# Key and query weights turned by DMAs straight from DRAM, and the order of the work as a table

## The chip, the cores and the metric

The kernel runs on one core of a Trainium2 chip. The time is the device time of one execution in microseconds (us), and less is better. The engines are TensorE (PE; its weight loads are shown apart as PEld), VectorE (DVE), ScalarE (ACT), GpSimd (POOL) and SyncE (SP). SP and ACT issue the DMAs of this kernel.

## The reference

Two layers, each made of a linear attention (A) and a gated feed-forward block (B), on one sequence of 2048 rows of 512 numbers in bfloat16. Each block reads a layer norm of x and adds its output to x. Both layers use the same weights.

```python
x = x + A(layernorm(x)); x = x + B(layernorm(x))      # twice

def A(x):                                  # 32 heads of 16
    q, k, v = split(x @ wqkv)              # wqkv: 512 x 1536
    pq, pk = q @ w_phi, k @ w_phi          # per head, 16 x 16
    phi_q = [softmax(pq), softmax(-pq)]    # over 16, so 32 features
    phi_k = [softmax(pk), softmax(-pk)]
    kv = phi_k.T @ v;  z = sum(phi_k)      # per head, over all 2048 rows
    return (phi_q @ kv) / (phi_q @ z + 1e-6) @ wo

def B(x):
    return (relu(x @ W_gate) * (x @ W_up)) @ W_down    # 512 -> 1376 -> 512
```

The sum kv runs over all rows, so no output of A exists before every row has had its keys and values.

## The kernel before

x stays in SBUF as 16 tiles of 128 rows, in 4 chunks of 4 tiles. A matmul needs the normalised tile turned (columns on the partitions). `Norm` takes the statistics of a tile (L385 on DVE, or a square on ACT, L408, with the sum taken in passing at L494), forms the reciprocal root on POOL (L393 to L444), normalises on ACT (L456), DVE or POOL (L468), and turns the tile by a DMA issued by SP, one tile (L486) or two at a time (L482), or by PE with a copy behind it (L478, L479).

The head matrices `w_phi` are multiplied into the weights first: `feature_weights` builds Wk2 = Wk x blockdiag(w_phi), and Wq2 likewise. The fold (L361) wants Wk and Wq turned. Wk is loaded with plain rows, turned by 16 small matmuls on PE (L348) and copied out of PSUM by ACT (L304) and DVE (L306); then come four folds and four casts into `Wk2`. Wq is loaded with plain rows (L238) and turned by two DMAs out of SBUF (L334). The block diagonal `Wblk` is made on DVE (L324) from w_phi and a mask `M8`.

Then, for each tile: keys (L637), the two exponentials (L642), values (L590) and their cast (L304), the sums of the features over 16 on DVE (L609 whole, L619 one sign at a time, L615 after a first addition on POOL, L606), reciprocal (L651), scaling on POOL or DVE (L657) and the running sum kv in PSUM (L679). Queries (L721, L725) have the same sums, a reciprocal (L730), a product (L732), scaling (L739) and a turn by DMA (L741). Attention (L758 to L809) and the feed-forward block (`glu`, L520 to L572) follow chunk by chunk. 17 matmuls of zeros (`wake`, L315) are given to PE at the start.

The order on every engine is fixed before the kernel runs. Each step is an `op` of a `Plan`, with the engine, an assumed duration, what it reads and writes and, for things that come from DRAM, an assumed time of arrival (`X_IN`, `WK_IN` and so on). Before, `Plan.order` played these durations through and let each engine take the ready step with the highest rank: the longest path to the end plus a number per group of steps (`RANK`). Strings in `STEP` say which engine takes which variant of a step (`kr0` is the way of the key sums of layer 0, tile by tile; `wev` the engine of each copy of the weights; `xm0` whether tiles are turned in pairs). Each engine runs its list in order, so a step that waits holds all behind it on that engine, DMA issues included.

Of the kernel before, what the change touches and what calls it, by code (L numbers as in the profile page):

```python
# [8 lines left out]
P = 128  # L9
# [51 lines left out]
class Plan:  # L61
# [10 lines left out]
    def op(self, eng, occ, fn, reads=(), writes=(), holds=(), lat=0.0, at=0.0, group=None, port=False, long=False):  # L72
# [4 lines left out]
        base, slope = RANK.get(f"{o.group}.{eng}") or RANK[o.group]  # L77
        o.bias = base - slope * o.i_in
# [19 lines left out]
    def order(self):  # L98
        for o in self.ops:
            for p in o.preds:  # L100
                p.succs.append(o)
        for o in reversed(self.ops):
            o.rank = o.cost + o.lat + max([s.rank + hop(o.eng, s.eng) for s in o.succs], default=0.0)
        free = {k: [0.0] * n for k, (pool, n) in self.kinds.items()}
        engines = sorted({o.eng for o in self.ops})
        busy = {e: 0.0 for e in engines}
        ready = {e: [] for e in engines}
        for o in self.ops:
            o.wait, o.t0 = len(o.preds), o.at
            if not o.wait:  # L110
                ready[o.eng].append(o)
        seq, left, now, shut = [], len(self.ops), 0.0, 0.0
        while left:
            moved, later = False, []
            for e in engines:
                if busy[e] > now + 1e-9:
                    later.append(busy[e])
                    continue
                best = None
                for o in ready[e]:  # L120
                    if o.t0 > now + 1e-9:
                        later.append(o.t0)
                        continue
                    if o.port and shut > now + 1e-9:
                        later.append(shut)
                        continue
                    ok = True
                    need = {}
                    for b in o.bufs:
                        if b.slot is None:  # L130
                            need[b.kind] = need.get(b.kind, 0) + 1
                    for k, n in need.items():
                        got = [t for t in free[k] if t is not None]
                        if len(got) < n:
                            ok = False
                        else:
                            t = sorted(got)[n - 1]
                            if t > now + 1e-9:
                                later.append(t)
                                ok = False  # L140
                    if ok and (best is None or (o.rank + o.bias, -o.i) > (best.rank + best.bias, -best.i)):
                        best = o
                if best is None:
                    continue
                o = best
                ready[e].remove(o)
                moved, left = True, left - 1
                o.start, end = now, now + o.cost
                busy[e] = now + o.occ
                if o.long:  # L150
                    shut = end
                later.append(busy[e])
                for b in o.bufs:
                    if b.slot is None:
                        b.slot = min((i for i, t in enumerate(free[b.kind]) if t is not None),
                                     key=lambda i: free[b.kind][i])
                        free[b.kind][b.slot] = None
                        b.end = 0.0
                    b.left -= 1
                    b.end = max(b.end, end + o.lat + FREE)  # L160
                    if not b.left:
                        free[b.kind][b.slot] = b.end
# [770 lines left out]
```

## Time and profile before

| | us |
|---|---|
| median of 3 runs | 382.19 (382.05 to 382.74) |
| profiled execution | 380.87 |
| its span, first to last instruction | 379.1 |
| PE busy | 368.0 |
| DVE busy | 272.1 |
| ACT busy | 211.0 |
| POOL busy | 139.5 |
| mean granted TensorE clock | 0.995 |

In the rows of the profile, `out<-in` names the tiles with their numbers left out: `b` stands for all buffers of the kinds b1, b2 and b4, `ps` for the PSUM banks, `Wk` and `Wq` for Wk2 and Wq2. A row of the timeline gives start, length, engine, line, operation and, in brackets, how long the engine had been idle and what ended that. A row of the table of stretches gives, for a stretch of time, its length, then for each engine the busy time with the number of instructions in parentheses, then the granted PE clock, the share of the DMA engines and GB/s. `SPq` and `ACTq` are the issuing of DMAs by SP and ACT, and a row of DMA issues ends with the time from issue to landing. Rows of groups give the busy time in all, the mean of one in ns, and the idle time before them.

### The profile page before, as it was taken

What the parts mean: (1) busy time and instruction counts of PE and PEld (TensorE: products, weight loads), DVE (VectorE), ACT (ScalarE), POOL (GpSimd) and SP (SyncE); (2) the same over time, 40 slices, a digit from 0 to 9 for tenths busy, and PEclk for the clock granted to TensorE, in tenths of its full rate; (3) what the DMA queues carried; (4) which work ended last, traced back from release to release, by engine and by line L of the source; (5) the groups of instructions that cost most, each with busy time, mean ns of one, the idle gap of its engine ahead of it and who ended that gap; (6) DMA issues with size and microseconds to landing.
All of it is one profiled execution on the core that took longest, in us unless ns stands there. A gap on an engine that the chain in (4) does not pass through costs nothing.

```text
span 379.1 us, 6873 instructions
## 1 busy us (share of the span) xinstructions
PE 368.0 (97%) x2435; PEld 190.8 (50%) x2435; DVE 272.1 (72%) x606; ACT 211.0 (56%) x436; POOL 139.5 (37%) x272
## 2 busy tenths in 40 slices
PE   8699999999999999999999999999999999999996
PEld 4245545666445454444454455576655444454444
DVE  5999999999789725636992688999985592532232
ACT  4899878752598241238476377986725135124600
POOL 3799876903366000134360446545311021000000
PEclk9899999999999999999999999999999999999999
DMA  8999816449585100141232020656977014020011
GB/s 255 252 219 212 211 39 138 47 91 173 96 153 100 29 15 2 28 57 29 47 52 55 3 55 2 124 104 86 164 153 112 0 28 112 0 28 30 1 43 55
DMA packets 98403, 32.23 MB, mean 85 GB/s; under 512 B 88800, under 2 KB 98368, under 8 KB 98368
## 3 DMA queue, kind: packets, MB, share of 16 engines
q1 hardware_dynamic: 94400, 28.36, 39.8%
q10 hardware_dynamic: 3968, 3.42, 2.9%
q8 instruction: 19, 0.31, 0.4%
q14 instruction: 16, 0.13, 0.1%
HBM read 8.44 MB, written 2.10 MB: 28 GB/s over the span
## 4 chain that ended last, share of the span: by engine, by line
PE 80%; DVE 9%; DMA 4%; POOL 4%; issue 1%; SPq 1%; ACT 0%; ACTq 0%; POOLq 0%
PE ps L540 36%; PE ps L572 19%; PE ps L809 6%; PE ps L721 4%; PE ps L590 4%; PE ps L637 3%; DMA b<-b 3%; PE ps L520 3%; PE q L758 2%; DVE sk L619 2%; POOL b L657 1%; PE ps L315 1%; DVE rk L651 1%; PE q L679 1%; DVE bnst L385 1%
## 5 line engine op out<-in xcount | busy, mean ns | idle before, releaser
L540 PE MATMUL ps<-b,wu 128*128 128x512 bf16 (+2 forms) x400 | 79.4, 337 | 0.0
L540 PE MATMUL ps<-b,wg 128*128 128x512 bf16 (+2 forms) x400 | 78.9, 337 | 0.0
L572 PE MATMUL ps<-wd,b 128*128 128x512 bf16 (+3 forms) x374 | 78.3, 367 | 0.0
L550 ACT CAST b<-ps 128x512 bf16<-128x512 f32 (+2 forms) x100 | 48.9, 505 | 40.6 <-PE ps L540 39.3
L553 DVE SCALAR_TENSOR_TENSOR b<-ps,b 128x512 bf16<-128x512 f32 (+2 forms) x60 | 34.9, 598 | 30.3 <-PE ps L540 29.8
L572 PEld LDWEIGHTS <-b 128*128 128x128 bf16 (+1 forms) x374 | 35.3, 98 | 39.4
L657 POOL TENSOR_TENSOR b<-b,rk 128x1024 bf16<-128x1024 bf16 (+6 forms) x30 | 42.1, 1410 | 33.9 <-DVE rk L651 26.0
L540 PEld LDWEIGHTS <-wg 128*128 128x128 bf16 x400 | 36.2, 98 | 32.9 <-issue 0.2
L540 PEld LDWEIGHTS <-wu 128*128 128x128 bf16 x400 | 36.1, 98 | 31.9
L456 ACT ACTIVATE b<-X,ve,rstd 128x512 bf16<-128x512 bf16 x42 | 33.4, 818 | 26.2 <-POOL ve L444 21.5
L739 POOL TENSOR_TENSOR b<-b,rq 128x512 bf16<-128x512 bf16 x25 | 26.3, 1050 | 31.2 <-DVE rq L732 24.2
L498 DVE TENSOR_TENSOR X<-X,ps 128x512 bf16<-128x512 bf16 (+2 forms) x34 | 22.0, 649 | 21.2 <-PE ps L572 20.6
L725 ACT ACTIVATE b<-ps 128x512 bf16<-128x512 f32 x64 | 33.3, 615 | 6.2 <-PE ps L721 6.1
L408 ACT ACTIVATE sq<-X 128x512 bf16<-128x512 bf16 x32 | 20.0, 626 | 28.5 <-DVE X L494 26.2
L637 PE MATMUL ps<-Wk,b 128*128 128x512 bf16 x128 | 31.5, 388 | 4.0 <-DMA b<-b 4.0
L642 ACT ACTIVATE b<-ps 128x512 bf16<-128x512 f32 x64 | 33.2, 612 | 1.2 <-PE ps L637 1.2
L494 DVE SCALAR_TENSOR_TENSOR X<-ps,X 128x512 bf16<-128x512 f32 x32 | 21.7, 684 | 13.4 <-PE ps L572 12.5
L809 PE MATMUL ps<-wo,b 128*128 128x512 bf16 x128 | 30.9, 379 | 0.1
L590 PE MATMUL ps<-wkv,b 128*128 128x512 bf16 x128 | 30.9, 384 | 0.0
L721 PE MATMUL ps<-Wq,b 128*128 128x512 bf16 x128 | 30.9, 379 | 0.0
L557 DVE TENSOR_TENSOR b<-b,b 128x512 bf16<-128x512 bf16 (+2 forms) x40 | 14.1, 373 | 22.3 <-ACT b L550 21.9
L546 ACT ACTIVATE b<-ps 128x512 bf16<-128x512 f32 (+2 forms) x40 | 19.8, 496 | 15.1 <-PE ps L540 15.1
(84 smaller groups left out, 463.8 us busy)
## 6 DMA issues: line engine op xcount, KB each, us to landing
out_dram<-X SPq DMA_DIRECT2D x15, 128.0 KB, 1.7
X<-in_A_x_dram ACTq DMA_DIRECT2D x3, 512.0 KB, 7.6
b<-b SPq DMA_TRANSPOSE x87, 3.2
wd<-in_B_W_down_dram SPq DMA_DIRECT2D x5, 256.0 KB, 3.2
wu<-in_B_W_up_dram SPq DMA_DIRECT2D x8, 160.0 KB, 3.3
wg<-in_B_W_gate_dram SPq DMA_DIRECT2D x8, 160.0 KB, 2.9
wkv<-in_A_wqkv_dram ACTq DMA_DIRECT2D x2, 512.0 KB, 5.1
wq<-in_A_wqkv_dram ACTq DMA_DIRECT2D x1, 512.0 KB, 8.3
```

What stands on the lines that cost most here:

```text
L456: pl.op("ACT", 0.72, lambda to=to, t=t, j=j: nc.scalar.activation(out=to(), in_=st.X[:, t, :], func=AF.Identity, scale=rstd[:, j:j + 1], b ...
L540: nc.tensor.matmul(ps[:], lhsT=wt[:, b, f * P:(f + 1) * P], rhs=xnT[:, lo:hi, b, :], start=(b == 0), stop=(b == NDB - 1))
L550: pl.op("ACT", 0.065 + 0.42 * share, lambda ups=ups, ru=ru: nc.scalar.copy(out=ru[:], in_=ups[:]), reads=[(ups, 0)], writes=[(ru, 0)])
L553: pl.op("DVE", 0.08 + 0.53 * share, lambda gps=gps, ru=ru, h=h, cs=cs: nc.vector.scalar_tensor_tensor(out=h[:, cs], in0=gps[:], scalar=0.0 ...
L572: nc.tensor.matmul(yps[:], lhsT=hs[f][:fsz, ti * P:(ti + 1) * P], rhs=st.wd[:fsz, f, cols], start=(f == 0), stop=(f == NFT - 1))
L590: nc.tensor.matmul(vp[:], lhsT=xnT[:, ti, kb, :], rhs=st.wkv[:, kb, D:2 * D], start=(kb == 0), stop=(kb == NDB - 1))
L637: nc.tensor.matmul(ps[:], lhsT=xnT[:, ti, kb, :], rhs=w(kb), start=(kb == 0), stop=(kb == NDB - 1))
L642: pl.op("ACT", 0.49, lambda s=s, ek=ek, pk=pk: nc.scalar.activation(out=ek[:, :, s, :], in_=pk[:].rearrange("p (j x) -> p j x", j=8), func ...
L657: eng.tensor_tensor(out=phiK[:, lo:hi, :, :].rearrange("p j s (f h) -> p (j s) f h", h=4), in0=ek[:, lo:hi, :, :].rearrange("p j s (f h) - ...
L721: nc.tensor.matmul(pq[:], lhsT=xnT[:, ti, kb, :], rhs=st.Wq2[:, kb, :], start=(kb == 0), stop=(kb == NDB - 1))
L725: pl.op("ACT", 0.49, lambda s=s, eq=eq, pq=pq: nc.scalar.activation(out=eq[:, :, s, :], in_=pq[:].rearrange("p (j x) -> p j x", j=8), func ...
L809: nc.tensor.matmul(yps[:], lhsT=turned(b), rhs=st.wo[:, b, :], start=(b == 0), stop=(b == NDB - 1))
```

## The change

- Wk is no longer loaded with plain rows. The first instruction of SP is a transposing DMA from `A_wqkv` in DRAM into `wkT`. The 16 turning matmuls and their four copies are gone, and the folds read `wkT`.
- Wq is no longer loaded with plain rows either. One transposing DMA from DRAM fills `wqT`, a buffer of kind b4. It and all loads that SP issues come after the turn of tile 5 (`turns`).
- The first two X tiles are loaded from ACT's queue instead of SP's; the value weights have a tile of their own, `wvt`.
- The order is a table, `ORDER`: the numbers of all 1867 steps in the order in which they are given out. `RANK` and the search for the best ready step are gone. Some assumed durations and arrivals differ.
- `STEP` differs: 19 wake matmuls instead of 17, of which the table sets eight ahead of the first fold and the others between the folds and among the first keys and values. Tiles 2, 3, 14 and 15 of the first norm are turned singly. In layer 0, the sums of keys and queries take POOL's first addition in 2 places fewer for keys and queries each (an addition per sign) and the one-sign form in more; three products of the queries (`qm0`) go to POOL, four in layer 1 (`qm1`); one normalisation goes from DVE to ACT. In the later norms, squares and normalisations change places between ACT and DVE, and one PE turn of layer 1 becomes a DMA.
- A further way of taking the sums ("T", a DMA turn and eight small matmuls with a mask `M8s`) is added; no letter T stands in the strings. The mask is made all the same, by one reduction on DVE.

```diff
-        base, slope = RANK.get(f"{o.group}.{eng}") or RANK[o.group]
-        o.bias = base - slope * o.i_in
...
+        assert sorted(ORDER) == list(range(len(self.ops)))
+        self.seq = [self.ops[i] for i in ORDER]
+        for o in self.seq:
...
-WF_IN, WK_IN, WV_IN, WQ_IN, LOADED = 3.5, 5.9, 8.6, 13.1, 13.0
-X_IN = [3.25, 3.8] + [7.0] * 2 + [10.1] * 4 + [11.6] * 4 + [14.5] * 4
+WF_IN, WK_IN, WV_IN, WQ_IN, LOADED = 3.6, 5.6, 8.25, 13.0, 13.0
+X_IN = [3.25, 5.2] + [6.75] * 2 + [9.75] * 4 + [11.25] * 4 + [12.75] * 4
...
-    nc.sync.dma_start(out=X[:, 0:1, :], in_=xv[:, 0:1, :])
+    nc.sync.dma_start_transpose(out=wkT[:], in_=A_wqkv[:, D:2 * D])
+    nc.scalar.dma_start(out=X[:, 0:1, :], in_=xv[:, 0:1, :])
     nc.scalar.dma_start(out=wf[:], in_=A_w_phi.rearrange("(b j) d f -> (j d) b f", b=NDB, j=8))
-    nc.sync.dma_start(out=X[:, 1:2, :], in_=xv[:, 1:2, :])
-    nc.scalar.dma_start(out=wkv[:, :, 0:D], in_=wv[:, :, D:2 * D])
+    nc.scalar.dma_start(out=X[:, 1:2, :], in_=xv[:, 1:2, :])
     nc.scalar.dma_start(out=X[:, 2:4, :], in_=xv[:, 2:4, :])
...
-    nc.scalar.dma_start(out=wkv[:, :, D:2 * D], in_=wv[:, :, 2 * D:3 * D])
+    nc.scalar.dma_start(out=wvt[:], in_=wv[:, :, 2 * D:3 * D])
     nc.scalar.dma_start(out=X[:, 4:8, :], in_=xv[:, 4:8, :])
     nc.scalar.dma_start(out=X[:, 8:12, :], in_=xv[:, 8:12, :])
-    nc.scalar.dma_start(out=wq[:], in_=wv[:, :, 0:D])
     nc.scalar.dma_start(out=X[:, 12:16, :], in_=xv[:, 12:16, :])
...
+    st.M8s = const.tile([P, 2, 4], BF16, name="M8s")
+    nc.vector.tensor_reduce(out=st.M8s[:], in_=ident[:].rearrange("p (z k h) -> p z h k", z=2, h=4), axis=AX.X, op=Alu.max)
...
+        if off:
+            part, deps = (lambda m, b: st.wkT[:, b, m * P:(m + 1) * P]), []
+        else:
+            wqT = Buf("b4", [P, NDB, D], BF16)
+            pl.op("SP", 2.0, lambda: nc.sync.dma_start_transpose(out=wqT[:], in_=st.wq_in),
+                  reads=[("turns", 1)], writes=[(wqT, 0)], at=at, lat=3.0)
+            part, deps = (lambda m, b: wqT[:, b, m * P:(m + 1) * P]), [(wqT, 0)]
...
-    "part0": "4111", "part1": "4111", "tB0": "A---", "tB1": "D-DA", "tA": "----", "wev": "AADDAAADADAAAAAA",
-    "xn1": "AAAAADAPDAADAADA", "turn": "A---", "wake": 17, "fuse0": "FFFA", "fuse1": "AFFA", "gate": 1, "sB0": 3,
-    "sB1": 2, "sA": 3, "xB0": "ADADAAAADADADDAA", "xB1": "DADAAADAAAAAAAAD", "xA": "AADDDDDADAADAAAA",
-    "xm0": "22222212", "xmB0": "22221122", "xmB1": "22222222", "xm1": "12222222", "om0": "11112222",
-    "om1": "11222222", "ev0": "AAAAAAAAAAAAAAAA", "ev1": "AAADAADAAAAAADAA", "ks0": "7888076880873788",
-    "ks1": "4322711876616443", "kr0": "H1111P1121221222", "kr1": "P12111111H12P222", "qr0": "1111H11P1122P1PP",
-    "qr1": "111P111111111112", "qs0": "PPPDPPPPDDDPDPPP", "qs1": "PPPPPPPDDPPPPPPP", "ot0": "DDDD-----DDDAA--",
-    "ot1": "--A---AD--A---D-",
+    "part0": "4111", "part1": "4111", "tB0": "A---", "tB1": "D-D-", "tA": "----", "wev": "AADDAAADADAAAAAA",
+    "xn1": "AAAAADAPDAADAAAA", "turn": "A---", "wake": 19, "fuse0": "FFFA", "fuse1": "AFFF", "gate": 1, "sB0": 4,
+    "sB1": 3, "sA": 2, "xB0": "ADADDAADDADADDDD", "xB1": "DADAAADDAAAAADAA", "xA": "AADDDDDAAADAAAAA",
+    "xm0": "11222211", "xmB0": "12222112", "xmB1": "22222221", "xm1": "12221212", "om0": "11112222",
+    "om1": "11222222", "ev0": "AAAAAAAAAAAAAAAA", "ev1": "AAADDAADAAAAAAAA", "ks0": "7888076880873788",
+    "ks1": "4321818154616442", "kr0": "H112121121122222", "kr1": "P111121112122212", "qm0": "DPDDDDDDDDPDDDPD",
+    "qm1": "DDDDPPDDDDPDDPDD", "qr0": "2111H1122121P1PP", "qr1": "111P112122111112", "qs0": "PPPPPPPPDDDPDPPD",
+    "qs1": "DDPDPPPPPPPPPPPP", "ot0": "DDDD------DDAA--", "ot1": "--A-DDAD---DD--A",
 }
-RANK = {
...
+ORDER = (
+    131, 144, 139, 143, 145, 129, 135, 130, 0, 1, 148, 149, 2, 3, 9, 4, 5, 150, 138, 10, 147, 152, 11, 13, 134, 12,
...
-        n = Norm(st, "b4", (1, 1, 2) if c == 0 else (2, 2), STEP["xn1"], STEP["xm0"], X_IN, STEP["turn"] if c == 0 else "")
+        n = Norm(st, "b4", (1, 1, 1, 1) if c == 0 else (2, 2), STEP["xn1"], STEP["xm0"], X_IN, STEP["turn"] if c == 0 else "")
```

`feature_sums`, with the added way "T":

```python
    if how == "T":
        turned = Buf("b2", [P, 8, P], BF16)
        pl.op("SP", 1.25, lambda: nc.sync.dma_start_transpose(out=turned[:], in_=e[:].rearrange("p j s x -> p (j s x)")),
              reads=[(e, 0), (e, 1)], writes=[(turned, 0)], lat=2.0, group=(group, t))
        ...
        pl.op("PE", 0.26, add_up, reads=[(turned, 0)], writes=[(sums, 0), (sums, 1)], group=(group, t))
        return
```

More of the change, by code (lines that the diff above doesn't have):

```diff
@@ L98, in order @@
     def order(self):
[L99 to L103, printed above, removed]
-        free = {k: [0.0] * n for k, (pool, n) in self.kinds.items()}
[L105 to L162, printed above, removed]
-                for s in o.succs:
-                    s.wait -= 1
-                    s.t0 = max(s.t0, end + o.lat + hop(e, s.eng))
-                    if not s.wait:
-                        ready[s.eng].append(s)
-                seq.append(o)
-            if not moved:
-                later = [t for t in later if t > now + 1e-9]
-                assert later, "the plan is stuck"
-                now = min(later)
@@ L176, in emit @@
+        return self.seq
     def emit(self):
```

98 lines of the change are left out of this document (49 added, 49 removed), and 112 rows, old and new, of tables (ORDER, RANK).

## The prediction

> **What bounds the kernel now.** I read the page first (busy rows, slices), then the chain that ended last, then a table of stretches, then PE's instructions in order of time.
>
> ```profile
> span 379.1 us, 6873 instructions
> PE 368.0 (97%) x2435; PEld 190.8 (50%) x2435; DVE 272.1 (72%) x606; ACT 211.0 (56%) x436; POOL 139.5 (37%) x272
> ...
> PE 80%; DVE 9%; DMA 4%; POOL 4%; issue 1%; SPq 1%; ACT 0%; ACTq 0%; POOLq 0%
> ...
> core 0: us, PE busy (x) PEld busy (x) DVE busy (x) ACT busy (x) POOL busy (x), PEclk, DMA share, GB/s
> ...
> 10.40:17.20 6.80, 3.47 (x13) 1.04 (x11) 6.17 (x19) 5.68 (x10) 5.84 (x13) 0.90 0.99 255
> 17.20:22.00 4.80, 4.75 (x24) 2.13 (x25) 4.41 (x11) 4.02 (x8) 4.55 (x9) 0.79 1.18 172
> 22.00:30.00 8.00, 7.20 (x61) 3.80 (x58) 7.53 (x14) 7.33 (x15) 7.77 (x12) 1.00 1.09 245
> 30.00:40.00 10.00, 10.00 (x67) 4.73 (x64) 9.38 (x16) 10.00 (x21) 9.66 (x9) 1.00 0.84 186
> 40.00:50.00 10.00, 9.87 (x102) 5.58 (x102) 10.00 (x21) 8.30 (x17) 7.97 (x5) 1.00 0.67 187
> 50.00:60.00 10.00, 8.90 (x66) 4.11 (x62) 10.00 (x23) 8.69 (x18) 7.99 (x9) 1.00 0.40 80
> 60.00:80.00 20.00, 19.16 (x206) 12.67 (x207) 19.09 (x53) 13.59 (x37) 12.91 (x30) 1.00 0.51 82
> ...
> 130.00:160.00 30.00, 30.00 (x165) 14.53 (x163) 14.56 (x26) 7.93 (x16) 1.51 (x5) 1.00 0.07 14
> ```
>
> PE is busy 97% of the span and 80% of the chain, but not everywhere the bound: the chain's 9% of DVE lie mostly before 60 us. From 130 us it has no hole to speak of: that part only shrinks with PE work. Before 80 us, DVE is as full as PE (10.00 of 10.00 us in both stretches from 40 to 60). PE's loss lies there: of the 69.6 us from 10.4 to 80, 6.25 are idle, and more pass at a lowered clock. By instruction:
>
> ```profile
> 6.59 1.06 PE L348 MATMUL ps<-ident,wkv 128*128 128x128 bf16 x16
> ...
> 10.43 1.02 PE L637 MATMUL ps<-Wk,b 128*128 128x512 bf16 x4
> 14.54 1.04 PE L637 MATMUL ps<-Wk,b 128*128 128x512 bf16 x4 [3.09 <-DMA b<-b]
> ...
> 52.72 0.43 PE L679 MATMUL q<-vext,b 128*128 128x68 bf16 x8 [0.54 <-POOL b L657]
> ...
> 60.14 0.41 PE L758 MATMUL q<-R,b 128*128 128x68 bf16 x8 [0.70 <-DVE b L778]
> ...
> 71.34 1.95 PE L540 MATMUL ps<-b,wu 128*128 128x128 bf16 x32
> ```
>
> The largest hole, 3.09 us, waits for the turned tile 1 of x. Why that is late stands in ACT's order (the first fence is from the timeline: start, length, instruction), and what follows on SP; the last row is a piece of the chain, the flight of the second half of Wq:
>
> ```profile
> 1.83 0.53 ACTq L228 DMA_DIRECT2D X<-in_A_x_dram  x1
> ...
> 4.30 0.98 ACTq L238 DMA_DIRECT2D wq<-in_A_wqkv_dram  x1
> ...
> 6.66 0.81 ACT L456 ACTIVATE b<-X,ve,rstd 128x512 bf16<-128x512 bf16 x1 [2.77 <-POOL ve L444]
> 7.38 1.53 ACT L304 COPY b<-ps 128x512 bf16<-128x512 bf16 x3
> 8.80 1.58 ACT L304 CAST Wk<-ps 128x512 bf16<-128x512 f32 x3
> 10.23 0.86 ACT L456 ACTIVATE b<-X,ve,rstd 128x512 bf16<-128x512 bf16 x1
> 11.11 1.29 SPq L486 DMA_TRANSPOSE b<-b  x1
> ...
> 16.71 2.67 SPq L334 DMA_TRANSPOSE b<-wq  x2
> ...
> 54.01 17.54 SPq L741 DMA_TRANSPOSE b<-b  x7
> ```
> ```profile
> 18.05 3.98 DMA b<-wq
> ```
>
> Tile 1 is normalised at 10.23 only, behind three copies (two of turned Wk, one of turned tile 0) and three casts of the folded Wk. The later waits are set by POOL and DVE (52.72, 60.14).
>
> **The change, part by part.** The sum is made against the profiled execution (380.87 us with 379.1 of span), which is 1.32 below the median of 382.19; I subtract the same gain from the median.
>
> Wk turned from DRAM. Gone: 16 turns on PE (1.06, all ahead of the first keys, so inside the start), two copies on ACT, two on DVE. New: one transposing DMA of 512 KB, first on SP. No row shows one from DRAM. Nearest: the two DMAs b<-wq, the same 512 KB out of SBUF, were issued from 16.71 and landed at 18.05 + 3.98 = 22.03, so 5.3 us. Issued at about 0.8, where SP's first load was, the new one lands near 6.1. Lower end: one of the two alone, 4.0, so 4.8. Upper end, since nothing shows a DRAM source: half that rate, 10.6, so 11.4 (an estimate from these two rows). I take 6.1, the row with the same bytes; the plain load was turned from 6.59.
>
> ACT's new order in the table is: cast of the first quarter of Wk, tile 0, tile 1, copy of turned tile 0, two casts. From 6.1: a fold of four small matmuls 0.4 (16 such took 1.06), a cast 0.53 (1.58 for three), two normalisations of 0.81: tile 1 is done near 8.7 (10.23 + 0.86 = 11.09 before). From there to K of tile 1 took 14.54 − 11.09 = 3.45, so that comes near 12.2 instead of 14.54, 2.3 us earlier. The other casts end near 10.4, so K of tile 0 stays where it is. Break-even for the landing is 6.1 + 2.3 = 8.4.
>
> First X tiles on ACT's queue, Wq's load gone from it. ACT issues four loads ahead of its first activation instead of three, 0.5 more (the 1.83 row), and four behind it instead of five, 0.98 less; ACT's first normalisation waited for POOL until 6.66, so neither shows. Tile 1 of X comes later, behind Wk, tile 0 and the small w_phi: between 0 and 1.5 us, taken as hidden, since its normalisation now has until 7.8; what outlasts that goes straight onto tile 1.
>
> Wake matmuls, 17 to 19, six or more of them now among the first keys and values. They cost nothing while PE waits there; if the holes are gone, 6 x 0.26 = 1.6 (four matmuls of this size in 1.04). They fill holes after which PE ran slow: (1 − 0.90) x 6.8 + (1 − 0.79) x 4.8 = 1.7 us lost between 10.4 and 22. The Trainium skill, "TensorE: Matmul & The Clock Gate" (Part 1), has the clock halved after about 3.4 us of idleness; the trace agrees in kind (3.09 us of hole, then 0.79). By that rule, with every hole split, all 1.7 would come back on PE.
>
> Wq turned from DRAM: one issue in place of two (2.67 on SP), placed behind the turn of tiles 4 and 5; 512 KB either way; 0, within 1 us either way, covered by the keys and values of tiles 2 to 5, which the table sets ahead of its fold. Weight loads: the same 28, now scattered, and the first behind the turn of tiles 4 and 5 and Wq's; two parts of the gate stand behind the first and second query transposes, one of down behind the fourth. Those seven began at 54.01 and took 2.5 each, and a load lands in about 3 (next row): the gate's last part by 62 against the first L540 at 71.34, down's by 67: 0.
>
> ```profile
> wg<-in_B_W_gate_dram SPq DMA_DIRECT2D x8, 160.0 KB, 2.9
> ```
>
> Tiles 2, 3, 14 and 15 turned singly instead of in pairs: two more SP issues of 1.29 (11.11 row), hidden in SP's waits; without that cover each costs 1.29 to the tiles behind it.
>
> Work moved between engines up to 80 us. Rows:
>
> ```profile
> L609 DVE TENSOR_REDUCE sk<-b 128x64 f32<-128x1024 bf16 x16 | 19.0, 1195 | 3.8 <-ACT b L642 3.8
> L619 DVE TENSOR_REDUCE sk<-b 128x32 f32<-128x512 bf16 x24 | 15.2, 658 | 0.4 <-ACT b L642 0.4
> L615 DVE TENSOR_REDUCE sk<-b 128x32 f32<-128x256 f32 x8 | 4.5, 568 | 0.2 <-POOL b L606 0.2
> L732 DVE TENSOR_TENSOR rq<-sq 128x32 bf16<-128x32 f32 x32 | 9.0, 282 | 0.1
> L306 DVE COPY b<-ps 128x512 bf16<-128x512 bf16 x8 | 3.1, 402 | 1.8 <-PE ps L348 1.8
> L468 DVE TENSOR_SCALAR b<-X,mv,rstd 128x512 bf16<-128x512 bf16 x7 | 2.8, 408 | 1.9 <-POOL rstd L395 1.9
> L265 DVE TENSOR_REDUCE M<-ident 128x4 bf16<-128x128 bf16 x1 | 0.3, 268 | 0.0
> L606 POOL TENSOR_TENSOR b<-b 128x256 f32<-128x256 bf16 x19 | 12.7, 679 | 0.4 <-ACT b L642 0.3
> L395 POOL TENSOR_TENSOR rstd<-ve,mhalf 128x2 f32<-128x2 f32 (+1 forms) x19 | 12.8, 673 | 0.1
> L444 POOL TENSOR_TENSOR ve<-u,rstd 128x2 f32<-128x2 f32 (+1 forms) x38 | 7.4, 194 | 1.8
> ```
>
> DVE: two copies less, −0.80; M8s, +0.27; one normalisation to ACT, −0.41; three products to POOL, −0.85; feature sums of keys and of queries, each one or so whole reduction and two half sums less for four single reductions: −1.195 − 2 x 0.568 + 4 x 0.658 = +0.30, twice. Sum −1.2. POOL: four additions less, −2.7; three products of 32 elements, between 0.19 and 0.68 each, taken as 0.2, the row nearest in size, +0.6; one more normalisation group, a power of 0.67 and three small ones of 0.2, +1.3; −0.8. ACT: two copies of 0.51 less, one normalisation of 0.81 more, −0.2. In the second half squares and normalisations move between ACT and DVE beside a full PE: 0, and one turn on PE less.
>
> The sum, from the engine that decides. On PE up to 5.0 come free: 2.3 (tile 1), 1.7 (clock), and about 1.0 of the later holes. But DVE must do its work before PE's stock of GLU matmuls opens at 71.34. It had 6.17 + 4.41 + 7.53 + 9.38 + 10 + 10 + 19.09 = 66.6 busy of 69.6: 3.0 idle, of which I let the earlier keys give half. 1.2 + 1.5 = 2.7 us. Profiled 378.2; median 382.19 − 2.7 = 379.5. Its own bounds: 1.2 (no idle closed) to 4.2 (all), so 378.0 to 381.0.
>
> **The rivals.** (1) Wk lands late, and slower is the end. Place: its cast heads ACT's queue, so tiles 0 and 1 are normalised behind it, and through the turn of tile 1 all of PE waits. It decides from a landing of 8.4 on. At 11.4 K of tile 1 is 3.0 later; less the 1.2 of DVE's work, +1.8: 384.0. For it: no row shows a source in DRAM, and wk competes with X. Against: b<-wq did as much beside other DMAs (the DMA share is 1.18 from 17.2 to 22). Chance 0.12. One page makes it far worse: the Trainium skill, "VectorE: DVE Perf Modes" (The three transpose paths), gives 1309 ns for a 128x128 block by DMA against 390 by TensorE. Estimated by it, 16 blocks in sequence take 20.9 us, Wk lands at 21.7, 13.3 behind the break-even, and the kernel takes 382.2 + 13.3 − 1.2 = 394.3; but b<-wq moved as many blocks in 5.3, so that rule gets 0.01.
>
> (2) Everything hidden: DVE paces the first 80 us wherever PE starts, and the new waits in DVE's order eat its 1.2. 381.0 to 382.6, taken as 381.9. For: 10.00 of 10.00 from 40 to 60. Against: 3.0 idle before. 0.16, half of it within 0.2%.
>
> (3) PE gets all: the table draws GLU work forward, so DVE's fullness costs nothing: 382.19 − 5.0 = 377.2. 0.12; against it, GLU's first matmuls need tile 0's attention, which needs the sums over all sixteen key tiles, and so all of DVE's key work.
>
> (4) The table puts PE behind late engines in the middle. Where there was no hole from 130 on, layer 1's keys now stand singly between GLU matmuls; ten waits like the 0.54 at 52.72 cost 5.4: 384.9. 0.10; against it, DVE has 15.4 us free from 130 to 160.
>
> **How the numbers follow.** The forecast holds 0.49. A measurement tells no change within 0.2%, 0.8 us (381.4 to 383.0). Faster: 0.49 + 0.12 + 0.08 = 0.69; same: 0.08 and a little of (1), 0.10; slower: the rest, 0.21. Range 376.8 to 383.8: it holds (3), (2) and the milder half of (1).
>
> **What would show it.** Right: no L348; the DMA of Wk landed by 7; K of tile 1 by 12.6; PEclk above 0.95 between 10 and 22; DVE still over 95% from 30 to 60; first L540 matmuls 2 to 3.5 us earlier. Wrong: landing after 8.4; first keys earlier but L540 not (2); PE holes after 130 (4); holes at GLU's first matmuls waiting for weight loads.

## The result, and the profile after

The changed kernel takes 384.02 us (median of 8 runs, 382.85 to 384.9); the kernel before took 382.12 beside it (8 runs, 381.5 to 383.69). The ratio is 1.0048, 95% interval 1.0031 to 1.0066: slower by half a per cent, where 379.5 was forecast. The profiled execution took 384.60, that of before 380.87, so the two traces stand 3.7 us apart where the medians stand 1.9 apart; a difference between two traces is read with that in mind all through this section.

The page of the changed kernel (line numbers are now those of its own file), and under it its stretches with the columns of the table shown of before, three wide ones added:

```profile
span 382.9 us, 6693 instructions
PE 366.5 (96%) x2384; PEld 190.5 (50%) x2417; DVE 274.9 (72%) x601; ACT 199.9 (52%) x428; POOL 136.6 (36%) x281
...
PE 81%; DMA 9%; ACT 2%; DVE 2%; issue 2%; POOL 2%; SPq 0%; ACTq 0%; POOLq 0%; DVEq 0%
```
```profile
10.40:17.20 6.80, 6.12 (x28) 2.49 (x28) 6.08 (x17) 5.23 (x10) 4.18 (x14) 1.00 0.54 138
17.20:22.00 4.80, 4.57 (x23) 1.89 (x21) 4.80 (x13) 3.70 (x8) 4.68 (x7) 1.00 1.06 165
...
10.40:22.00 11.60, 10.69 (x49) 4.37 (x49) 10.88 (x29) 8.93 (x17) 8.87 (x20) 1.00 0.76 149
22.00:130.00 108.00, 100.36 (x775) 55.47 (x785) 94.06 (x214) 75.90 (x165) 61.16 (x104) 1.00 0.62 122
130.00:375.00 245.00, 242.87 (x1496) 123.97 (x1514) 161.30 (x337) 110.66 (x241) 61.40 (x135) 1.00 0.29 54
```

The same three wide stretches of the kernel before:

```profile
10.40:22.00 11.60, 8.22 (x37) 3.18 (x36) 10.58 (x28) 9.70 (x17) 10.39 (x21) 0.85 1.07 220
22.00:130.00 108.00, 104.47 (x804) 57.16 (x801) 99.77 (x227) 77.28 (x167) 66.20 (x109) 1.00 0.65 128
130.00:375.00 245.00, 244.89 (x1522) 124.60 (x1520) 154.28 (x327) 118.83 (x244) 59.29 (x124) 1.00 0.29 52
```

PE does less (366.5 against 368.0 busy). Of the chain that ended last, DVE's share fell from 9% to 2%, and that of the DMAs rose from 4% to 9%. PE's idle time, the length of a stretch less its busy time, went from 3.38 to 0.91 between 10.4 and 22, with the clock back at 1.00. That is the gain. From 22 to 130 it went from 3.53 to 7.64, and from 130 to 375 from 0.11 to 2.13; a new wait of 1.60 stands ahead of 10.4. Sum: −2.47 + 4.11 + 2.02 + 1.60 = +5.3, less 1.5 of busy time: the 3.8 by which the span grew.

The main holes in PE's order of time in the changed kernel, each with what ended it, and the first keys (L575) and values (L516); the rows are taken from several views:

```profile
6.43 0.59 PE L287 MATMUL ps<-Wblk,wkT 128*128 128x128 bf16 x4 [1.60 <-DVE Wblk L269]
...
11.27 1.03 PE L575 MATMUL ps<-Wk,b 128*128 128x512 bf16 x4
...
13.14 1.04 PE L516 MATMUL ps<-wvt,b 128*128 128x512 bf16 x4 [0.62 <-DMA b<-b]
14.01 1.89 PE L575 MATMUL ps<-Wk,b 128*128 128x512 bf16 x7
...
26.53 1.90 PE L575 MATMUL ps<-Wk,b 128*128 128x512 bf16 x7 [1.19 <-DMA b<-b]
...
36.68 0.60 PE L575 MATMUL ps<-Wk,b 128*128 128x512 bf16 x2 [0.99 <-DMA b<-b]
109.23 1.04 PE L575 MATMUL ps<-Wk,b 128*128 128x512 bf16 x4 [0.99 <-DMA b<-b]
225.91 1.04 PE L575 MATMUL ps<-Wk,b 128*128 128x512 bf16 x4 [1.01 <-DMA b<-b]
```

Four holes of about one microsecond wait for a turned tile (`DMA b<-b`). Two more, at 54.32 (0.88, POOL) and 61.90 (0.86, ACT), wait for late engines. The turns that end the four are slow ones: issued at 21.81, 31.98, 105.15 and 221.58, they land 4.68, 4.66, 4.03 and 4.28 later, where most of their kind take 2.4 (one tile) or 3.1 (two). Why they are slow is what the experiments had to find.

The start, in a row of DVE's timeline and three of the page's DMA issues (KB each, us from issue to landing):

```profile
5.52 0.76 DVE L269 TENSOR_TENSOR Wblk<-M,wf 128x256 bf16<-128x256 bf16 x2 [1.16 <-DMA wf<-in_A_w_phi_dram]
```
```profile
wkT<-in_A_wqkv_dram SPq DMA_TRANSPOSE x1, 4.8
wf<-in_A_w_phi_dram ACTq DMA_DIRECT2D x1, 16.0 KB, 4.2
b<-in_A_wqkv_dram SPq DMA_TRANSPOSE x1, 5.2
```

Wk is there early, at 5.60. But the 16 KB of w_phi, issued 0.4 behind the turn, need 4.2 us instead of 2.4 and land at 5.42 instead of 3.20, so the first fold starts at 6.43 and the keys of tile 0 at 11.27, 0.84 later than before. PE's first work on tile 1 (its values, then its keys at 14.01) begins at 13.14 instead of 14.54.

### The profile page after: what moved, and what is told of

The parts are those of the page before. It is cut to its first block, busy times and chain, and to the rows that moved or that the text cites. A ratio compares the mean times of both kernels' runs of the same rounds, so it can differ in the third digit from the quotient of the medians.

```text
span 382.9 us, 6693 instructions
## 1 busy us (share of the span) xinstructions
PE 366.5 (96%) x2384; PEld 190.5 (50%) x2417; DVE 274.9 (72%) x601; ACT 199.9 (52%) x428; POOL 136.6 (36%) x281
## 4 chain that ended last, share of the span: by engine, by line
PE 81%; DMA 9%; ACT 2%; DVE 2%; issue 2%; POOL 2%; SPq 0%; ACTq 0%; POOLq 0%; DVEq 0%
PE ps L466 36%; PE ps L498 16%; DMA b<-b 7%; PE ps L751 7%; PE ps L575 5%; PE ps L659 5%; PE ps L516 5%; PE ps L446 2%; PE q L700 2%; PE q L617 1%; DMA wf<-in_A_w_phi_dram 1%; ACT b L580 1%; DVE sk L556 1%; ACT b L382 1%; POOL b L595 0%
## 5 line engine op out<-in xcount | busy, mean ns | idle before, releaser
L479 DVE SCALAR_TENSOR_TENSOR b<-ps,b 128x512 bf16<-128x512 f32 (+2 forms) x70 | 40.5, 605 | 36.5 <-PE ps L466 25.5
L595 POOL TENSOR_TENSOR b<-b,rk 128x1024 bf16<-128x1024 bf16 (+7 forms) x30 | 41.0, 1381 | 45.0 <-DVE rk L589 30.4
L580 ACT ACTIVATE b<-ps 128x512 bf16<-128x512 f32 x64 | 35.9, 613 | 16.2 <-PE ps L575 15.8
L382 ACT ACTIVATE b<-X,ve,rstd 128x512 bf16<-128x512 bf16 x39 | 31.6, 823 | 16.4 <-POOL ve L370 16.4
L663 ACT ACTIVATE b<-ps 128x512 bf16<-128x512 f32 x64 | 34.9, 615 | 8.3 <-PE ps L659 7.2
L575 PE MATMUL ps<-Wk,b 128*128 128x512 bf16 x125 | 31.8, 379 | 4.6 <-DMA b<-b 4.4
L420 DVE SCALAR_TENSOR_TENSOR X<-ps,X 128x512 bf16<-128x512 f32 x36 | 24.3, 681 | 16.0 <-PE ps L498 8.3
L424 DVE TENSOR_TENSOR X<-X,ps 128x512 bf16<-128x512 bf16 (+2 forms) x30 | 19.3, 648 | 21.7 <-PE ps L498 16.1
L334 ACT ACTIVATE sq<-X 128x512 bf16<-128x512 bf16 x36 | 22.9, 636 | 18.8 <-DVE X L420 18.5
L516 PE MATMUL ps<-wvt,b 128*128 128x512 bf16 x124 | 31.8, 379 | 0.9 <-DMA b<-b 0.6
L546 DVE TENSOR_REDUCE sq<-b 128x64 f32<-128x1024 bf16 x19 | 22.5, 1199 | 0.0
L720 DVE TENSOR_TENSOR b<-q,dd 128x512 bf16<-128x512 f32 x32 | 21.8, 681 | 0.3
```

Source lines behind the costliest of these rows:

```text
L382: pl.op("ACT", 0.72, lambda to=to, t=t, j=j: nc.scalar.activation(out=to(), in_=st.X[:, t, :], func=AF.Identity, scale=rstd[:, j:j + 1], b ...
L479: pl.op("DVE", 0.08 + 0.53 * share, lambda gps=gps, ru=ru, h=h, cs=cs: nc.vector.scalar_tensor_tensor(out=h[:, cs], in0=gps[:], scalar=0.0 ...
L516: nc.tensor.matmul(vp[:], lhsT=xnT[:, ti, kb, :], rhs=st.wvt[:, kb, :], start=(kb == 0), stop=(kb == NDB - 1))
L575: nc.tensor.matmul(ps[:], lhsT=xnT[:, ti, kb, :], rhs=w(kb), start=(kb == 0), stop=(kb == NDB - 1))
L580: pl.op("ACT", 0.49, lambda s=s, ek=ek, pk=pk: nc.scalar.activation(out=ek[:, :, s, :], in_=pk[:].rearrange("p (j x) -> p j x", j=8), func ...
L595: eng.tensor_tensor(out=phiK[:, lo:hi, :, :].rearrange("p j s (f h) -> p (j s) f h", h=4), in0=ek[:, lo:hi, :, :].rearrange("p j s (f h) - ...
```

## The experiments

Names of the theories: **T**, the table's order puts PE behind turned tiles and late engines; **S**, the start with turns from DRAM is worse and the loss stays to the end; **D**, loads and Wq's 512 KB in flight slow the turns of x. **C** came up on the way: reads of TensorE's own code slow the turns. Ratios are to the kernel before, run beside each.

### The parts without the table, and the parts one by one

e1: the changed kernel with the old planner. `order()` and `RANK` of the kernel before take the place of the table:

```diff
-        self.seq = [self.ops[i] for i in ORDER]
+        # before's search for the best ready step, with RANK
```

> All parts of the change but the table: the order comes from the list planner and its RANK numbers as before. Theory T (the table puts PE behind turned tiles and other engines from 22 us on): PE's idle time between 22 and 110 us falls from 6.5 us to below 4, and the time is 381 to 382.5, at least 1.5 below the changed kernel's 384.0. Theory S (the start with the turns from DRAM is worse, and its delay is carried to the end): the start is the same, so 384 or more.

Measured: 388.21, ratio 1.0149 (1.0118 to 1.0179). T's number is missed: the old planner does not bring the parts below before's time, and PE's idle time from 22 to 110 is 5.87, not under 4. S's (384 or more) is met. In its trace the largest hole, which the changed kernel does not have, stands in the second layer's feed-forward:

```profile
266.29 0.82 PE L522 MATMUL ps<-b,wu 128*128 128x384 bf16 x4 [2.40 <-DMA b<-b]
```

(The code in the next two fences is shortened.) e2 and e3: the kernel before with Wk alone, then Wk and Wq, from DRAM, planned anew by the old planner.

```diff
+    nc.sync.dma_start_transpose(out=wkT[:], in_=A_wqkv[:, D:2 * D])
...
+    pl.op("SP", 2.0, lambda: nc.sync.dma_start_transpose(out=wqT[:], in_=st.wq_in), ...)   # e3
```

> The kernel before with one part of the change: Wk turned from DRAM by SP's first DMA, the first X tiles on ACT's queue; old planner, old strings, Wq as before. Theory T: tile 1's turn lands 1 us earlier or more, and the time is 380.5 to 382.1, not above before. Theory S: w_phi lands near 5.4, the first fold comes after 6.3, and the time is 383 to 384.5.

> As the run with Wk alone, and Wq turned from DRAM too, behind the turn of tile 5, with the weight loads behind that turn as well. Theory T: within 0.8 of the run with Wk alone. Theory S: 383.5 to 385. A third one, D (the 512 KB of Wq's turn in flight slow the turns of tiles 6 to 9 behind it): 0.5 to 1.5 above the run with Wk alone, with PE waiting for a turn near 26 us.

Measured: 395.65 (1.0361, 1.0332 to 1.0390) and 393.79 (1.0307, 1.0261 to 1.0353), above every theory. PE's waits say why (e2, then e3; us in total, times, longest):

```profile
PE q L671 <- POOL b L649: 4.9, 4, 2.3
PE q L671 <- DVE b L649: 3.1, 2, 2.0
```
```profile
PE q L667 <- DVE b L645: 4.5, 1, 4.5
```

The sums kv wait for scaled keys. With eight steps fewer the same `RANK` numbers give another order on ACT, DVE and POOL all the way down. So e1 to e3 compare orders and not parts. The next runs hold the order fixed.

e4: the changed kernel with w_phi first on ACT's queue and a longer wake ahead of the first fold.

```diff
+    nc.scalar.dma_start(out=wf[:], ...)
     nc.scalar.dma_start(out=X[:, 0:1, :], in_=xv[:, 0:1, :])
-    nc.scalar.dma_start(out=wf[:], ...)
```

> The changed kernel with its table, but w_phi is loaded ahead of tile 0 of X on ACT's queue, and one of the wake matmuls ahead of the first fold is five long, so that PE is busy until the fold. Theory T: the first fold comes 0.7 us earlier and PE runs at full clock through the folds, but the later waits keep most of it: 383.2 to 384. Theory S: the gain is carried to the end: 381.5 to 382.8.

Measured: 384.66 (1.0063, 1.0040 to 1.0085), above both ranges: the edit did not bring the start forward. w_phi now landed at 2.84, but X tile 0, second in the queue, at 5.06 instead of 2.99, and Wk at 6.26; the first fold began at 7.25 instead of 6.43. In the runs with Wk's turn first, a load issued with it lands in 2.1 to 2.6, and the three behind it take 3.6 to 5.3. The turn of tile 1 was issued 0.8 later than in the changed kernel and the span of the trace grew by 0.2: in this one run a shift of the start is mostly eaten by later waits, against S.

### One part at a time in the order before

f1 and f2 keep every step of the old plan, so that the same order comes out; the steps that fall away issue nothing. f1 has Wk from DRAM and X tiles 0 and 1 on ACT's queue. f2 has Wq from DRAM alone, at the place of its first SBUF turn. f4 is f1 with X tile 0 ahead of Wk's turn on SP and w_phi first on ACT.

```diff
-                pl.op("PE", 4 * TR, tr, writes=[(tps, 0)], holds=(w,), at=at)
+                pl.op("PE", 4 * TR, lambda: None, writes=[(tps, 0)], holds=(w,), at=at)    # f1, f4
...
+                pl.op("SP", 1.25, (lambda: nc.sync.dma_start_transpose(out=st.wqT[:], in_=st.wq_in))
+                      if m == 0 else (lambda: None), writes=[(wt[m], 0)], at=at, lat=1.85)  # f2
```

> The kernel before, in its own order on every engine, with one thing changed: Wk is turned by a DMA straight from DRAM (first on SP), X tiles 0 and 1 stand on ScalarE's queue, and the 16 turns on TensorE with their four copies are gone. Theory T (the table puts PE behind turned tiles and late engines): the parts are good, so this is faster than before: tile 1 normalised some 0.7 to 1.6 us earlier, two DVE copies less, 380.3 to 381.8. Theory S (the start with DRAM turns is worse): w_phi lands at 5.4 instead of 3.2, the first fold near 6.4, and the kernel is not faster than before, 382 to 384. Theory D (weight loads and Wq in flight slow the turns of x) says nothing new here: as T.

> The kernel before, in its own order on every engine, with only Wq turned by one DMA from DRAM at the place of the first of its two SBUF turns; its load is gone. The prediction and T: 0 within 1 us, 381.2 to 383.2. D: the 512 KB from DRAM hold up the turns issued behind it by one to two us, PE waits for a turned tile between 20 and 30 us: 383 to 384.5. S: nothing.

> As f1, with X tile 0 ahead of Wk's turn on SP and w_phi first on ScalarE's queue (both landed near 3 where they stood ahead of the turn). S: w_phi near 2.9 brings the first fold to Wk's landing, about 6.2, and this is 0.3 to 1 us faster than f1. T: start shifts of this size are eaten by later waits: within 0.4 of f1.

Measured: f1 384.94 (1.0076, 1.0048 to 1.0104), f2 381.61 (0.9978, 0.9959 to 0.9997), f4 389.19 (1.0184, 1.0152 to 1.0216).

f2: Wq's part is right as forecast, and D's extra microsecond isn't there. It is the only kernel here that beats both, 0.22% faster than before. In its trace the gain stands at the start, where Wq's load is no longer in flight: the turn of tile 1 takes 2.51 instead of 3.38, the hole ahead of tile 1's keys is 2.22 instead of 3.09, and the granted clock stays at 1.00 from 10.4 to 22.

f1 is slower than S allowed. Its first loss is the start: in this order DVE's `Wblk` stands ahead of tile 0's statistics, waits for w_phi until 5.78 (4.04 before), and tile 0 is normalised at 8.30 instead of 6.66. But two more holes stand 90 and 200 us behind anything that was edited, where before had 0.65 and none:

```profile
110.91 1.04 PE L635 MATMUL ps<-Wk,b 128*128 128x512 bf16 x4 [1.33 <-DMA b<-b]
...
225.82 1.04 PE L635 MATMUL ps<-Wk,b 128*128 128x512 bf16 x4 [1.20 <-DMA b<-b]
```

f4 misses both expectations by over 3 us. It says what a turn from DRAM costs where loads are ahead of it. Issued 0.45 us later than in f1, behind two small loads, it takes 10.3 us instead of 5.1:

```profile
X<-in_A_x_dram SPq DMA_DIRECT2D x1, 128.0 KB, 2.3
...
wf<-in_A_w_phi_dram ACTq DMA_DIRECT2D x1, 16.0 KB, 2.5
wkT<-in_A_wqkv_dram SPq DMA_TRANSPOSE x1, 10.3
```

### Loads out of the way of the turns

f3: the changed kernel with all 28 weight loads of SP behind the turn of tile 15.

```diff
-ORDER = (... 98, 99, 100, 103, 118, ...)          # loads are steps 101 to 128, scattered
+ORDER = (... 98, 99, 100, 101, 102, ... 128, ...)
```

> The changed kernel with one thing moved: its 28 weight loads on SP all stand behind the turn of tile 15 instead of between the turns. D: the turns of tiles 6 to 13 take 2.5 to 3.3 us instead of 4.3 to 5.1, the two holes of PE at 26.5 (1.19) and 36.7 (0.99) go, and 1 to 2.5 us come back: 381.5 to 383. T: the holes only move to other late engines (VectorE is 9.9 of 10 busy from 30 to 40), 383.4 to 384.6.

Measured: 388.31 (1.0159, 1.0128 to 1.0191), above both ranges. The first half of D holds: of the hole at 26.5, 0.23 is left, and the one at 36.7 is gone. But the loads now stand ahead of the turns of the queries, on SP and in the DMA engines; the first two of these take 6.9 and 5.9 us, and PE waits:

```profile
63.35 0.64 PE L700 MATMUL q<-R,b 128*128 128x68 bf16 x8 [5.15 <-DMA b<-b]
```

### Where the slow turns come from

In the stretch of the changed kernel that ends in the hole at 225.91 no load is in flight. This is the DMA view of 221.5 to 225.9 (busy tenths and GB/s in 40 slices, two of its queues), and under it the issue of the view of 221.5 to 222, the turn itself:

```profile
DMA  0000700000029999995000000021000000015999
GB/s 0 0 0 0 149 0 0 0 0 0 0 49 202 235 212 216 149 116 9 7 16 9 9 16 0 2 10 7 0 0 0 0 0 0 0 26 102 191 209 200
...
q8 instruction: 1, 0.02, 1.9%
q14 instruction: 1, 0.01, 1.4%
```
```profile
b<-b SPq DMA_TRANSPOSE x1, 4.3
```

The turn's bytes go at 200 GB/s for 0.7 us, then almost nothing moves for nearly 2 us, and the landing is reported 4.28 after the issue, which itself took 2.1 instead of 1.2. Beside it run a packet of queue q8 (16 KB, from 221.98, for 1.30 us) and one of queue q14 (8 KB): code. Queue q8 has 19 packets in this run, and from one to the next PE starts 253 weight loads and matmuls in the mean (249 to 253 in all traces); with 192 instructions more on PE (g4 and h3 below) there are 20 packets. So q8 brings PE's code. What happens inside the DMA engines the trace doesn't show. I took all turns issued between 80 and 345 us in the 19 traces of this study and sorted them by whether a code packet was in flight with them (one that ended 0.3 us or more after the turn's issue and began before its landing):

| code in flight | turns | median us | longest us | over 3.5 us |
|---|---|---|---|---|
| none | 1008 | 3.05 | 3.48 | 0 |
| PE's (16 KB) | 304 | 3.79 | 5.41 | 196 |
| another queue's (8 KB) alone | 163 | 3.25 | 4.31 | 42 |

No weight load is in flight in that part of the run. Of the two holes before 40, where loads are, the one at 26.5 has both beside its turn: a read of PE's code from 23.05, 1.62 long, and loads. With the loads moved (f3) the turn takes 3.72 instead of 4.68; with the read elsewhere and the loads in place (g2 below) it takes 3.26, and the hole is gone. At 36.7 the loads suffice: in e4 they alone stand beside the same turn, and it takes 4.29.

f1 has 32 instructions fewer on PE than before (16 turns with their weight loads), so all its later code packets come at other places in the work. g1 puts 32 back: 16 one-column matmuls among the first wakes of f1. g2, g3 and g4 put 64, 128 and 192 into the first eight wakes of the changed kernel, and narrow the last matmul of each of these.

```diff
-        pl.op("PE", ..., lambda z=z: nc.tensor.matmul(z[:], lhsT=st.zero[:, 0:P], rhs=st.zero[:], ...), ...)
+        def zeros(z=z, widths=(1,) * 4 + (320,) if i < 8 else (D,)):      # g2; g1 2 + 448, g3 8 + 192, g4 12 + 64
+            for w in widths:
+                nc.tensor.matmul(z[:, 0:w], lhsT=st.zero[:, 0:P], rhs=st.zero[:, 0:w], start=True, stop=True)
```

> The kernel of f1 (the order before, Wk alone from DRAM) with 16 one-column matmuls among the first wakes, 32 instructions, so that TensorE's stream is as long as before's. Theory C (blocks of 16 KB of TensorE's code, one per 256 instructions, are read by the DMA engines that turn tiles; a turn beside such a read lands 0.6 to 1.8 us later, and the 32 instructions that fell away moved which turns are hit): the holes at 110.9 (1.33) and 225.8 (1.20) go back to 0.7 and under 0.3, and the time goes from 384.9 to 382.5 to 383.7; what is left is the later start. Theory S (the late start is all of it, and it stays to the end): 384.5 to 385.5.

> The changed kernel with 64 more instructions on TensorE, 32 one-column matmuls among its first eight wakes, which are shorter for it; nothing else. C: the turns issued at 57.8, 105.2 and 221.6 are no longer beside a read of code and the holes at 109.2 (0.99) and 225.9 (1.01) go: 381.8 to 383.3. T and D (order, or weight loads beside the turns): no change, 383.5 to 384.6.

> As g2 with 128 instructions more (64 one-column matmuls). C: the turns at 105.2 and 221.6 are free as well, other turns are hit, which mostly land before they are needed: 381.5 to 383.5. T and D: 383.5 to 384.6.

> As g2 with 192 instructions more (96 one-column matmuls). C: the reads come beside the turns issued near 108.7 and 226.6, next to those that hurt: 382.3 to 384.5. T and D: 383.5 to 384.6.

Measured: g1 383.73 (1.0039, 1.0021 to 1.0058), g2 383.75 (1.0042, 1.0023 to 1.0061), g3 387.13 (1.0132, 1.0100 to 1.0164), g4 385.37 (1.0083, 1.0057 to 1.0108).

g1's median is 1.2 us under f1's, for 32 instructions that compute nothing (the intervals overlap a little, so the size is rough), and 0.03 above C's range. The hole at 225.8 is gone; the turn ahead of it takes 2.4 us where it took 4.2 in f1 (f1's row, then g1's):

```profile
b<-b SPq DMA_TRANSPOSE x1, 4.2
```
```profile
b<-b SPq DMA_TRANSPOSE x1, 2.4
```

The other one is 1.01 (at 107.48) instead of 1.33: another packet, at 104.73, stands beside that turn. So C accounts for the hole at 225.8. The rest of f1 (1.0039 in g1) is not S's alone: g1 has two holes that before has not in that size, 1.33 at 59.93 and 0.82 at 283.20, and both wait for turns, of 4.73 and 4.60 us, with a read of PE's code beside them (57.80 and 280.32).

g2 to g4 all miss C's numbers: I had followed the turns that would come free, and not priced those that would be hit instead. g2's hole at 225.9 is gone, but there is one of 1.52 at 82.45, and the one at 109, which C had expected to go, is 1.30 with another read beside its turn; so it falls into T's and D's range. g3 shows C best. Its first code packet comes at 13.0 us instead of 23.1, on the turn of tile 1, which all of PE waits for. That turn, issued at 9.73, takes 5.4 us (3.7 in the changed kernel):

```profile
15.20 1.04 PE L518 MATMUL ps<-wvt,b 128*128 128x512 bf16 x4 [2.63 <-DMA b<-b]
```

The hole was 0.62 there. In g4 the packet comes at 12.15, the turn takes 5.1 and the hole is 1.99. Not all of it is the packet: in g2, with none beside it, the turn takes 4.05, and the last load of x, which the turn shares the DMA engines with, landed at 13.21 in g3 and 12.65 in the changed kernel. The paddings move the changed kernel over 3.4 us, more than the 1.9 in question. So the kernel before had to be seen at other places too. h1, h2 and h3 are the kernel before with the same three paddings.

> The kernel before with 64 more instructions on TensorE: 32 one-column matmuls among its first eight wakes, which are shorter for it; nothing else. Theory C (reads of TensorE's code beside turns in flight; before's own place in the blocks is a good one): other turns are hit, 382.5 to 385. Theory T (the table's order is what costs; code reads hit both kernels alike and matter little to before): 381.7 to 383.0 in all three.

> As h1 with 128 more. C: the first read comes near 13, on the turn of tile 1 (issued 11.1, PE waits for it): 383 to 386. T: 381.7 to 383.0.

> As h1 with 192 more. C: the first read comes near 12, also beside the turn of tile 1: 383 to 386. T: 381.7 to 383.0. The mean of before's four places against the mean of the changed kernel's four (384.0, 383.8, 387.1, 385.4: 385.1) says what the change costs without the luck of the code's place: C, under 1.5 us; T, over 2 us.

Measured: h1 384.23 (1.0053, 1.0033 to 1.0073), h2 383.55 (1.0029, 1.0013 to 1.0045), h3 385.15 (1.0060, 1.0039 to 1.0081). All three are slower than before itself, in C's ranges and outside T's; the hole ahead of tile 1's keys, 3.09 before, is 3.83, 4.00 and 2.40. For h2 and h3 that is luck, not C: their first packets come at 10.22 and 7.54, not near 13 and 12, and are over at 11.36 and 8.63, when the turn of tile 1 has just been issued (11.32) or is not yet (12.64); only h1's, at 13.48, stands beside it. In these kernels the padding also moved the start. The turns of Wk on PE, from 6.59 and 1.06 long before, begin at 7.18, 6.83 and 7.19 and take 1.25, 1.06 and, in h3,

```profile
7.19 1.91 PE L350 MATMUL ps<-ident,wkv 128*128 128x128 bf16 x16
```

and the turn of tile 1 is issued at 11.87, 11.32 and 12.64 instead of 11.11. How much of the 0.3 to 0.6% is the place of the code and how much the altered wakes, no run here separates. By place of the code (added instructions; the idle time is that of PE from 22 to 130 us, 108 less the busy time of that row):

| | +0 | +64 | +128 | +192 | mean |
|---|---|---|---|---|---|
| kernel before, ratio | 1.0000 | 1.0053 | 1.0029 | 1.0060 | 1.0036 |
| changed kernel, ratio | 1.0048 | 1.0042 | 1.0132 | 1.0083 | 1.0076 |
| kernel before, idle us | 3.53 | 4.75 | 3.81 | 4.52 | 4.15 |
| changed kernel, idle us | 7.64 | 6.02 | 6.11 | 5.31 | 6.27 |

The means lie 0.40%, 1.5 us, apart, between C's bound (under 1.5) and T's (over 2), and the four ratios of a row spread more than that: the times alone don't settle whether the change costs anything once the code's place is averaged out. The idle time from 22 to 130 does not overlap: the changed kernel is behind there at each of the four places, by 4.11, 1.27, 2.30 and 0.79, 2.1 us in the mean. Each of these figures is of one execution, though, and the four profiled ones of the changed kernel took 0.5 us more in the mean than their medians, those of before 0.2 less. From 130 to 375 it is the other way, 1.76 against 2.37 in the mean; the 0.11 of the kernel before, which the prediction took for a stretch without holes, was luck: h1 and h3 have 3.43 and 4.18.

k1 and k2 ask how much of the 2.1 is loads. Nine weight loads, issued from 25.8 to 31.4 ahead of a turn that PE waits for, go behind the last load and behind two query turns; k2 adds g2's 64 instructions.

```diff
-ORDER = (... 121, ... 117, 113, 127, ... 76, 109, ... 119, 123, ... 112, ... 125, 88, ...)
+ORDER = (... 76, ... 88, ... 101, 121, 117, 113, 109, 119, 112, ... 368, 127, 123, ... 378, 125, ...)
```

> The changed kernel with nine of its weight loads moved on SP, those issued between 25.8 and 31.4, ahead of a turn that TensorE waits for: six (gate and up) go behind the last load near 47.6, three (down) behind the fourth and fifth query turns. TensorE's code stays in place. D (loads beside the turns are a part of the loss between 22 and 130 us): the turn issued near 32 takes about 2.5 us instead of 4.66, the hole at 36.7 (0.99) goes, TensorE's idle time from 22 to 130 falls from 7.6 to 5.5 to 6.5, and 382.6 to 383.5 us. T (the order of the other engines sets it): the idle time stays above 7, 383.6 to 384.6.

> k1 with the 64 instructions more on TensorE of g2, to see the same move at another place of the code. D: less than g2's 383.75 by 0.5 to 1.4, idle from 22 to 130 under 5.5 where g2 had 6.0. T: 383.4 to 384.2.

Measured: k1 383.85 (1.0039, 1.0023 to 1.0056), k2 382.95 (1.0043, 1.0020 to 1.0066). In the traces the turn takes 2.4 instead of 4.7, the hole at 36.7 is gone, and k1's PE is idle for 5.70 from 22 to 130 instead of 7.64, k2's for 4.08 instead of g2's 6.02. The turn and its hole are D's part; the idle time of k1 is not proof of it, because e4, which moved no weight load, has 5.77 there:

```profile
22.00:130.00 108.00, 102.30 (x790) 55.94 (x789) 94.68 (x215) 76.04 (x166) 60.87 (x104) 1.00 0.61 123
```
```profile
22.00:130.00 108.00, 102.23 (x789) 55.79 (x788) 94.51 (x214) 76.72 (x166) 61.52 (x104) 1.00 0.58 121
```

(k1, then e4.) In time it is not: both ratios agree with those without the move (1.0048 and 1.0042), k1's median lies in T's range, k2's in D's. What stays in all six traces of the changed order that were compared (changed, g2, g3, g4, k1, k2) is T's part: a wait of 0.88 to 1.00 near 53 to 56 for POOL's scaled keys, where before had 0.54, and one of 0.85 or 0.86 near 61 to 64 for ACT's exponentials of the queries, where before waited 0.70 for DVE.

## Why the prediction was wrong

**Wk's landing, 6.1 (4.8 to 11.4).** Right: 5.60 here, and 5.9 in f1. Rival (1) did not come true. The rule given with it, the Trainium skill's 1309 ns for a block in sequence ("VectorE: DVE Perf Modes", The three transpose paths), is off by a factor of four here (20.9 us for 16 blocks against 4.8). But the upper end was real: behind two small loads the same DMA took 10.3 (f4, one run).

**Tile 1 and tile 0.** Half right. Tile 1 was normalised by 9.36 (8.7 forecast) and its turn issued at 9.39, so PE's first work on it came 1.4 us earlier than before, not 2.3 (its keys, at 14.01, 0.5 earlier); tile 0's keys came 0.84 later, not at the same time. The step that failed at the start is "First X tiles on ACT's queue ... so neither shows": I costed the issue time on ACT and the later X tile 1 at nothing, and did not cost what a turn from DRAM does to the loads issued just behind it. The price is in the `wf` row: 2.4 became 4.2, and w_phi gates the fold.

**The clock and the wakes.** Right. The granted clock is 1.00 from 10.4 to 22 (0.90 and 0.79 before). The Trainium skill, "TensorE: Matmul & The Clock Gate" (Part 1), ties a halved clock to about 3.4 us of idleness; here the longest hole after the first fold is 1.19 and no lowered clock follows, which agrees; the kernel before fell to 0.79 after 3.09, a little less than that figure.

**Wq, 0 within 1.** Right: f2, 0.9978.

**Weight loads scattered, 0.** Wrong in the trace, hardly so in the time. I asked only whether they come in time for their users, not what they do to the turns they stand among: 4.66 instead of 2.4 for the one issued at 31.98. Moving nine of them took that hole away and brought 0.2 and 0.8 us in the medians, which the intervals don't tell from nothing.

**DVE's work, −1.2 by 80 us.** Wrong. DVE's busy time between 10.4 and 80 was 66.6 before and is 66.7 now. Of the listed parts the sums came as worked out (36 reductions of 31.2 us before, 39 of 31.8 after), but only one product of the queries had left DVE by 80, not three, and small scalings of keys cost 353 ns each instead of 196.

**The sum.** This is the step that failed most. The forecast let PE's stock of work open earlier by 2.7, and let the later holes of PE only shrink ("about 1.0 of the later holes", nothing lost from 130 on). Of the 2.7, 1.2 was DVE's work, which did not fall (+0.1), and 1.5 was half of DVE's 3.0 of idle time, of which 2.9 are left. The first large feed-forward matmuls began at 72.62 instead of 71.34. The later holes grew: PE's idle time from 22 to 375 went from 3.64 to 9.77, 4.11 more of it before 130, and the largest of its waits are for turned tiles that land in 4.0 to 4.7 us. So what the start had won was lost there: rival (4) in kind, with its place wrong. I put its waits behind 130 us and on late engines; the runs have most of them from 22 to 130 and on turned tiles. That its 384.9, with a chance of 0.10, was near the 384.02 measured is luck: it was made of ten waits behind 130.

**What no step had.** That 32 or 36 fewer instructions on PE move the reads of its code, and with them which turns are slow, 200 us on. The waits that the prediction took as hidden rest on turns that land as fast as in the kernel before, and one turn in five between 80 and 345 us (304 of 1475) has a read of PE's code beside it. The kernel before is the fastest of its four versions; the three others are 0.3 to 0.6% slower, by the place of the code and the altered wakes together.

Left open: how much of the half per cent is the change itself. The idle time from 22 to 130 says 2.1 us in the mean of the four places (0.8 to 4.1, one execution each), that from 22 to 375 says 1.5; the times say 1.5, with a spread as large. As the paddings also delayed the start of the kernel before, its mean may be too high and the 1.5 too low. No run here brought the changed order down to the time of the kernel before.

## What to carry to other kernels

Before a fraction of a per cent is put down to an edit, move the code of both kernels by a few dozen harmless instructions and compare over the places. A transfer on which an engine waits should have slack for a code read beside it, about 1.8 us here (4.2 against 2.4 in f1 and g1), and a large transposing DMA should be issued with nothing small and urgent behind it or ahead of it. Priorities such as `RANK` hold for the list of steps they were set for (e2 and e3); to test one part, keep the list and empty the steps.

## What the runs showed of the hardware

- A read of TensorE's code, 16 KB in one packet for every 250 or so of its weight loads and matmuls, lengthens a DMA turn beside it: median 3.79 against 3.05 us, up to 5.41, and no turn without one over 3.48 of 1008. The Trainium skill, "Runtime: NRT & Kernel Launch" (Instruction fetch mechanics), has the 256 instructions to 16 KiB, which agrees with the 19 packets here, and calls the cost of crossing such a block "mostly hidden"; here it is not hidden from the turns, and the changed kernel's medians at four places of its code lie up to 3.4 us apart.
- A 512 KB turn from DRAM takes 4.8 to 5.5 us where it is issued first, 5.2 to 6.4 as Wq's among the turns, and 10.3 behind 144 KB of loads issued 0.45 us earlier (one run). The 16 KB of w_phi issued 0.4 us behind it take 3.6 to 4.7 us instead of 2.4.
